# A preLN memory-attention and MLP kernel: how block 0's last-row values are laid out, pieces of the output weights, when norms and additions may start, and the length of a block's instruction stream

## The chip, the cores and the metric

The kernel runs on one core of a Trainium2 chip. The core has a matrix engine (PE, with its weight loads shown as PEld), a vector engine (DVE), an activation engine (ACT), a general engine (POOL) and an engine that issues DMAs (SP). Each runs its own list of instructions in order; they wait for one another through semaphores. The metric is the device time of one execution in microseconds, from runs on the chip. One execution was taken with the profiler.

## The reference

One sequence of 2048 tokens with 512 channels goes through an attention layer whose memory is carried from segment to segment, and then through an MLP, each behind a layernorm and with a residual:

```python
for s in range(n_seg):                                   # 64 segments of 32 tokens
    h = jnp.concatenate([mem, xs], axis=1)               # 8 memory rows + 32 tokens
    q, k, v = h @ Wq, h @ Wk, h @ Wv                     # 32 heads of 128
    p = softmax(where(mask, q k^T * scale, -1e9))
    o = einsum('bhte,hed->btd', p v, Wo)
    mem = o[:, :M, :]                                    # memory of the next segment
    outs.append(o[:, M:, :])
h  = x + A(layernorm(x))
h2 = h + (gelu(layernorm(h) @ w1 + b1) @ w2 + b2)        # 512 -> 1792 -> 512
```

The memory makes the segments a recurrence: segment s + 1 can't project its 8 memory rows before the output projection of segment s is done.

## The kernel before

**A planner.** The program is first recorded as a list of operations (`Sched.op`, L87), each with engine, duration, keys that it reads and writes, and, for PE, a place in a PE order that is written out by hand (`START` L50 for segment 0, `ORDER` L45 for the others). `schedule` (L166) lays the operations of the other engines out by a list scheduler: priority is the longest way to the end plus a bonus by the kind of result (`BONUS`, L31), and a copy that ACT or DVE could do (`either`) goes where it ends first. DMAs on SP are laid out with durations of 0.07 + KB/390 us (L142). `finalize` (L257) works out the semaphore waits: an operation waits for the last needed operation of each engine, unless its engine knows already that it is past. Waits beyond the first of a PE operation are moved up to an earlier operation without one, or become instructions of their own. `align` (L329) can put extra weight loads (pads) into the projection passes, so that the instruction count reaches a wanted phase modulo 256; before, `PHASE` is empty and only `LEAD` = 60 pads stand at the program's start.

**Segments and blocks.** Four segments make a block of 128 tokens (`bk`, `sg`). Each segment's pack A holds 24 rows of tokens and the 8 memory rows; the last 8 tokens of the four segments of a block are packed together as pack B and projected once a block. For segment s, PE runs (L45): passes of Q, K and V for both halves of the heads (`passes` L680, 4 matmuls of 512 columns for each of 4 channel chunks), scores SC (L826), the products PV for the memory and last rows (`pv_c` L863), PVA, the products of the 24 token rows of the segment before (`pv_a` L924), F, the projections of the next block's pack B, in segment 3 of a block instead the output projection of the last rows of the block before (`wo_B` L982), the output projection WO in two halves (`wo_units` L949), and the scores SA of the token rows (L892). WO's result is transposed into TT (L971), and two additions (L965) make the next segment's memory rows hT from it.

**Last-row values.** V of pack B comes as VSB, one row per token of the block. The products need it laid out in another way, VBD. `v_B_spread` (L783) writes VSB to a DRAM tensor v_last in four DMAs and reads it back in four others. For block 0 these eight DMAs are put by hand into SP's chain of weight loads (L1286): writes behind the fourth WK load, reads two WQ loads later.

**Weights.** WV, WK, WQ and WO come in four DMAs of 1 MB each (L606, L621). WO's unit q waits for two of the four pieces (L962). In START the WO of segment 0 is taken in two halves, with pack B's second Q projection and `warm`, 12 matmuls that compute nothing, between them.

**From attention to MLP.** `nat` (L998) puts a finished block together: a DMA transpose and four small DMAs into oN, on DVE the addition to x (L1006) and the statistics, on POOL rs2 (L1012, L1013), and a DMA to h_mid. While segments 54 to 60 run, `EARLY` (L43) starts the MLP of the first four blocks: `hx_early` (L1096) loads a row of h_mid into xT and normalizes it on DVE (L1098), `hn_early` (L1101) transposes the result by DMA; both wait for a named place in PE's order. Behind the last segment come w1 (L1109, L1317) and w2 (L1324) in four superblocks of 512 tokens. `p2_res` (L1063) adds b2 to the residual on POOL (L1066); it waits for all uses of WV and for rs2 of the last block. DVE adds this to PE's sum (L1387), and only then may PE use that bank for the next superblock.

Of the kernel before, what the change touches and what calls it, by code (L numbers as in the profile page):

```python
# [30 lines left out]
BONUS = {"": 5.14, "EC0": -5.14, "EC1": -4.67, "KA0": 6.35, "KA1": 9.81, "KB0": -1.33, "KB1": 2.96, "OTB": -1.22, "OTm0": 40, "OTm1": -40,  # L31
# [11 lines left out]
EARLY = {54: (("hx", 0, 0.1), ("hx", 1, 0.6)), 55: (("hn", 0, 0.1), ("hn", 1, 0.4), ("hx", 2, 0.8)), 56: (("hx", 3, 0.3), ("hn", 2, 0.7)),  # L43
         57: (("hn", 3, 0.1), ("w1", 0, 0.6)), 58: (("w1", 6, 0.2),), 59: (("w1", 1, 0.1), ("w1", 2, 0.8)), 60: (("w1", 3, 0.2), ("w1", 4, 0.5), ("w1", 5, 0.8))}
# [10 lines left out]
class Op:  # L55
# [3 lines left out]
    def __init__(self, eng, fn, reads, writes, name, dur, mode):  # L59
# [15 lines left out]
class Sched:  # L75
# [181 lines left out]
    def finalize(self):  # L257
# [64 lines left out]
        for e in engs:  # L322
            c = 0
# [1122 lines left out]
```

## Time and profile before

| what | value |
|---|---|
| median of 3 runs | 868.45 us (867.11 to 869.06) |
| profiled execution, its own time | 870.69 us |
| its span, first to last instruction | 869.0 us |
| mean granted PE clock | 0.984 |
| idle time of DVE, ACT | 32%, 38% of the span |
| bytes read from and written to HBM | 31.34 and 8.39 MB |
| first TT transpose, last one of 66 | at 53.8 us, at 771.8 us |

The profile's page gives busy time by engine, the DMA rate in slices and the costliest groups. The table of waits tells for each engine which line waited and what ended the wait; "issue" stands where no semaphore that the profile shows ended it. The chain of waits follows the work that ended last back through what released it. A timeline lists instructions in order of time, with the idle time before them and its releaser in brackets.

### The profile page before, as it was taken

How to read it: one execution, taken by the hardware profiler on the slowest of the kernel's cores; microseconds unless marked ns; L12 is line 12 of the kernel's file. 1: busy time of each engine (PE TensorE's matmuls, PEld its weight loads, DVE VectorE, ACT ScalarE, POOL GpSimd, SP SyncE). 2: the span in 40 equal slices, each digit the busy share in tenths (PEclk: the TensorE clock that was granted, in tenths of full speed). 3: DMA queues.
4: the chain of work that ended last, by engine and by line, in shares of the span. 5: the costliest groups of instructions: out<-in, count | busy, mean ns of one | idle time of the engine just before them, and what ended most of it. 6: DMA issues, size and time to landing. Idle time of an engine off the chain costs nothing.

```text
span 869.0 us, 46364 instructions
## 1 busy us (share of the span) xinstructions
PE 810.0 (93%) x21588; PEld 408.0 (47%) x20389; DVE 587.9 (68%) x1852; ACT 542.8 (62%) x1570; POOL 87.0 (10%) x206
## 2 busy tenths in 40 slices
PE   4688999999999999999999999999998999987998
PEld 1244454445455555454555545544553544442443
DVE  3277778788787878787878787777776878634111
ACT  2346676767676767676767776767775776632332
POOL 3021000101000000000000101000000000006200
PEclk9799999999999999999999999999999999998999
DMA  9961010201010111111110111010112130363200
GB/s 351 356 180 21 4 34 17 41 17 40 18 31 26 29 29 28 30 24 33 21 38 19 40 19 33 13 32 11 35 41 47 34 96 16 77 184 91 61 25 25
DMA packets 68033, 49.27 MB, mean 57 GB/s; under 512 B 29044, under 2 KB 64252, under 8 KB 67836
## 3 DMA queue, kind: packets, MB, share of 16 engines
q1 hardware_dynamic: 67504, 46.03, 18.9%
q8 instruction: 165, 2.70, 1.3%
q10 hardware_dynamic: 332, 0.27, 0.1%
q14 instruction: 32, 0.26, 0.1%
HBM read 31.34 MB, written 8.39 MB: 46 GB/s over the span
## 4 chain that ended last, share of the span: by engine, by line
PE 82%; DMA 6%; DVE 5%; ACT 3%; issue 2%; SPq 1%; POOL 1%; ACTq 0%; DVEq 0%
PE ps L695 37%; PE ps L959 14%; PE ps L447 7%; PE quad L1324 4%; PE ps L1317 4%; PE ps L988 3%; PE quad L871 3%; PE quad L840 2%; PE ps L902 2%; DMA WK<-in_B_w_dram 2%; PE quad L931 2%; PE ps L840 1%; ACT kq L713 1%; DMA WQ<-in_A_Wq_dram 1%; POOL WV L1066 1%
## 5 line engine op out<-in xcount | busy, mean ns | idle before, releaser
L959 PE MATMUL ps<-WO,OT 128*32 128x256 bf16 x4224 | 142.7, 275 | 6.8 <-issue 4.2
L713 ACT CAST OT<-quad 128x128 bf16<-128x128 f32 x191 | 84.0, 440 | 96.5 <-PE quad L875 96.0
L959 PEld LDWEIGHTS ps<-WO,OT 128*32 128x32 bf16 x4224 | 104.3, 97 | 55.6 <-DVE rsc L856 25.1
L695 PE MATMUL ps<-WQ,hT 128*32 128x512 bf16 x1796 | 123.4, 385 | 5.0 <-DVE hT L965 4.6
L695 PE MATMUL ps<-WK,hT 128*32 128x512 bf16 x1544 | 121.3, 385 | 0.0
L695 PE MATMUL ps<-WV,hT 128*32 128x512 bf16 x1528 | 118.5, 380 | 0.0
L713 ACT CAST kq<-ps 128x512 bf16<-128x512 f32 x158 | 92.4, 585 | 40.2 <-PE ps L695 39.5
L714 ACT ACTIVATE kq<-ps 128x512 bf16<-128x512 f32 x160 | 94.4, 590 | 24.5 <-PE ps L695 24.3
L736 DVE STREAM_TRANSPOSE KALL<-kq 128x256 f32<-128x256 f32 x160 | 69.0, 438 | 23.6 <-ACT kq L713 22.8
L971 DVE STREAM_TRANSPOSE TT<-ps 128x256 f32<-128x256 f32 x66 | 29.7, 450 | 79.7 <-PE ps L959 79.5
L757 POOL COPY ZC<-QTB 128x256 bf16<-128x256 bf16 x64 | 26.4, 414 | 509.9 <-PE ps L840 319.1
L695 PEld LDWEIGHTS ps<-WQ,hT 128*32 128x32 bf16 x1796 | 45.4, 97 | 54.4 <-issue 22.3
L1320 ACT ACTIVATE WQ<-ps,b1t 128x512 bf16<-128x512 f32 x42 | 28.9, 687 | 62.8 <-PE ps L1317 62.8
L736 DVE STREAM_TRANSPOSE QT<-kq 128x256 f32<-128x256 f32 x128 | 57.0, 445 | 15.5 <-ACT kq L714 10.9
L695 PEld LDWEIGHTS ps<-WK,hT 128*32 128x32 bf16 x1544 | 40.6, 98 | 55.8 <-issue 40.2
L695 PEld LDWEIGHTS ps<-WV,hT 128*32 128x32 bf16 x1528 | 40.3, 97 | 52.0 <-issue 29.5
L447 PE MATMUL ps<-WV,hT 128*32 128x512 bf16 x520 | 53.4, 382 | 0.0
L1387 DVE TENSOR_TENSOR WV<-quad,WV 128x512 bf16<-128x512 f32 x16 | 11.1, 692 | 62.5 <-PE quad L1324 54.9
L447 PE MATMUL ps<-WK,hT 128*32 128x512 bf16 x504 | 51.1, 381 | 0.0
L853 ACT ACTIVATE EC<-ps,nmc 128x64 f32<-128x64 f32 x130 | 39.5, 309 | 18.5 <-DVE nmc L849 18.4
L1324 PE MATMUL quad<-WK,WQ 128*128 128x512 bf16 x164 | 42.5, 388 | 5.5 <-DVE WV L1387 5.3
L713 DVE CAST VS<-ps 128x512 bf16<-128x512 f32 x64 | 42.8, 669 | 5.5 <-PE ps L447 5.5
(154 smaller groups left out, 1398.0 us busy)
## 6 DMA issues: line engine op xcount, KB each, us to landing
WV<-in_A_Wv_dram SPq DMA_DIRECT2D x4, 1024.0 KB, 12.7
WK<-in_A_Wk_dram SPq DMA_DIRECT2D x4, 1024.0 KB, 18.2
v_last<-VSB SPq DMA_DIRECT2D x64, 64.0 KB, 2.1
WQ<-in_A_Wq_dram SPq DMA_DIRECT2D x4, 1024.0 KB, 7.9
VBD<-v_last SPq DMA_DIRECT2D x64, 64.0 KB, 2.0
WO<-in_A_Wo_dram SPq DMA_DIRECT2D x4, 1024.0 KB, 15.2
h_mid<-xr SPq DMA_DIRECT2D x16, 128.0 KB, 1.8
WQ<-h_mid SPq DMA_DIRECT2D x4, 512.0 KB, 4.2
```

The costliest lines, as they stand in the source:

```text
L447: return e.add_instruction(mybir.InstMatmult(name="I-%d" % (4000000 + _kept[0]), engine=mybir.EngineType.PE, start_tensor_calc=start, stop ...
L695: ins = e.matmul(o, l, m, start=(k == 0), stop=(k == DC - 1), tile_position=(0, 32 * j), skip_group_check=True)
L713: return {"act": (lambda e: e.copy(out, src), t_act(n, ps_)), "dve": (lambda e: e.tensor_copy(out, src), 0.16 + 1.042e-3 * n * fast)}
L714: return {"act": (lambda e: e.mul(out, src, scale_), t_act(n, ps_)), "dve": (lambda e: e.tensor_scalar(out, src, scale_, None, ALU.mult), ...
L736: S.op("dve", lambda e: e.transpose(out, src), reads=[("kq", i)], writes=[key], dur=t_dve(256) + 0.02)
L757: S.op("pool", lambda e: e.tensor_copy(dst, src), reads=[("QTB", bk % 2, q) for q in range(2)], writes=[("ZCb", par)], dur=0.45)
L853: ins = e.activation(EC[:, r, sl, :], o[:, 64 * sl:64 * sl + 64], ACTF.Exp, bias=nmc[:, r, sl:sl + 1], accum_out=smc[:, r, sl:sl + 1])
L959: ins = e.matmul(ps[bank][32 * j:32 * j + 32, 0:256], lhs(slot(h)), wo_cols(h, b), start=(k == 0), stop=(k == 15), tile_position=(0, 32 * ...
L971: S.op("dve", lambda e: e.transpose(tt.rearrange("p c q t -> p (c q t)"), ps[bank][:, 0:256]), reads=[("ps", bank)], writes=[("TT", par)], ...
L1317: ins = e.matmul(ps[bank][:, 0:SBT], W1[:, cc, fc * P:(fc + 1) * P], hnT_of(k)[:, cc, :], start=(cc == 0), stop=(cc == DC - 1))
L1320: S.op("act", lambda e: e.activation(gT[:, fc, :], ps[bank][:, 0:SBT], ACTF.Gelu_apprx_tanh, bias=b1t[:, fc:fc + 1], scale=1.0), reads=[(" ...
L1324: S.op("pe", lambda e: e.matmul(quad[:, t, :], gT_of(k, fc)[:, t * P:(t + 1) * P], W2[:, fc, :], start=(fc == 0), stop=(fc == FC - 1)), re ...
```

## The change

Last-row values of block 0 are now laid out by PE. POOL builds masks of ones (`turn`, in the unused half of OTB), and 16 matmuls with them move VSB's rows to their places; two copies bring the result to VBD. The eight DMAs of block 0 are gone from SP's chain; the other blocks keep theirs. WO comes in eight pieces of 512 KB, and each WO unit waits for the two pieces that it reads; START takes segment 0's WO in four parts, with 8 + 8 warm matmuls. `pv_a` becomes two operations, each waiting for its own half of V. The early norm moves from `hx_early` to `hn_early`, with a PE place of its own, and the loads start at segment 51. The b2 additions of superblock 0 no longer wait for rs2. The planner gets SP durations for each kind of DMA (`occ`), drops waits that another wait of the same operation implies, and has new bonuses for nearly every kind; `align` pads the PE stream at the first segment of each block from block 1 on to the phase 92, so that a block is a multiple of 256 instructions, and `LEAD` is 0. `JOIN` and `RECORD` are empty: what they would switch stays off.

```diff
+TURN = 1.27
-PHASE = ()
+LOCK = 92
+JOIN = 0
+RECORD = ()
-LATE, RAW, LEAD = 0, 10, 60
+LATE, RAW, LEAD = 0, 10, 0
-BONUS = {"": 5.14, "EC0": -5.14, "EC1": -4.67, "KA0": 6.35, "KA1": 9.81, "KB0": -1.33, "KB1": 2.96, "OTB": -1.22, "OTm0": 40, "OTm1": -40,
+BONUS = {"": 40, "EC0": -0.86, "EC1": 0.35, "KA0": -40, "KA1": 2.87, "KB0": -40, "OTB": -0.07, "OTm0": 0.99, "OTm1": -3.04, "OTx": -40, "PA": -19.24,
...
-EARLY = {54: (("hx", 0, 0.1), ("hx", 1, 0.6)), 55: (("hn", 0, 0.1), ("hn", 1, 0.4), ("hx", 2, 0.8)), 56: (("hx", 3, 0.3), ("hn", 2, 0.7)),
-         57: (("hn", 3, 0.1), ("w1", 0, 0.6)), 58: (("w1", 6, 0.2),), 59: (("w1", 1, 0.1), ("w1", 2, 0.8)), 60: (("w1", 3, 0.2), ("w1", 4, 0.5), ("w1", 5, 0.8))}
+EARLY = {51: (("hx", 0, 0.2),), 52: (("hn", 0, 0.2), ("hx", 1, 0.6)), 53: (("hn", 1, 0.2), ("hx", 2, 0.6)), 54: (("hn", 2, 0.2), ("hx", 3, 0.6)),
+         55: (("hn", 3, 0.2),), 57: (("w1", 0, 0.6),), 58: (("w1", 6, 0.2),), 59: (("w1", 1, 0.1), ("w1", 2, 0.8)), 60: (("w1", 3, 0.2), ("w1", 4, 0.5), ("w1", 5, 0.8))}
-START = (("B", "V", 0, (0, 6), (1, 7)), "V", "X", ("B", "V", 1, (0, 6), (1, 7)), ("B", "K", 0, (0, 4), (1, 6)), "K0", "K1", ("B", "K", 1, (0, 4), (1, 6)),
-         ("B", "Q", 0, (0, 5)), "Q0", ("B", "Q", 0, (1, 4)), "Q1", "Z", "SC0", "SC1", ("B", "Q", 1, (0, 5)), "PV0", "PV1", "SA", "WO", ("T", "WO", 0, 4),
-         ("B", "Q", 1, (1, 6)), ("W", 7, 12), ("T", "WO", 4, 8))
+START = (("B", "V", 0, (0, 6), (1, 7)), "V", "Y", "X", ("B", "V", 1, (0, 6), (1, 7)), ("B", "K", 0, (0, 4), (1, 6)), "K0", "K1", ("B", "K", 1, (0, 4), (1, 6)),
+         ("B", "Q", 0, (0, 5)), "Q0", ("B", "Q", 0, (1, 4)), "Q1", "Z", "SC0", "SC1", ("B", "Q", 1, (0, 5)), "PV0", "PV1", "SA", "WO", ("T", "WO", 0, 2),
+         ("B", "Q", 1, (1, 6)), ("T", "WO", 2, 4), ("W", 7, 8), ("T", "WO", 4, 6), ("W", 7, 8), ("T", "WO", 6, 8))
...
-        o = self.op(eng, fn, reads, writes, {"sp": 0.07 + kb / 390.0, "act": 0.1}.get(eng, 1.0), 0, name, list(after) + [old])
+        o = self.op(eng, fn, reads, writes, {"sp": max(occ, 0.07 + kb / 390.0), "act": 0.1}.get(eng, 1.0), 0, name, list(after) + [old])
...
+            waits = [p for p in waits if not any(q is not p and snap[q][p.eng] >= p.idx for q in waits)]
...
-            if PHASE and o.tag is not None and o.tag[0] != seg:
+            if LOCK is not None and o.tag is not None and o.tag[0] != seg:
                 seg = o.tag[0]
-                owed = (PHASE[seg % 4] - at) % FETCH_N
-                if owed > FETCH_N - SLIP:
-                    owed = 0
+                if seg % 4 == 0:
+                    owed = (LOCK - at) % FETCH_N
+                    if owed > FETCH_N - SLIP:
+                        owed = 0
...
         for g in range(4):
-            load(lambda e, g=g: e.dma_start(WO[:, g * 8:(g + 1) * 8, :], wo_d[:, g * 8:(g + 1) * 8, :]), 1180, [("WO", g)])
+            for a in range(2):
+                h0 = 16 * (g // 2) + 8 * a + 4 * (g % 2)
+                load(lambda e, h0=h0: e.dma_start(WO[:, h0:h0 + 4, :], wo_d[:, h0:h0 + 4, :]), 590, [("WO", g, a)])
...
-            if r == 1:
+            if r == 1 and bk > 0:
                 v_B_spread(bk)
...
+        def turn_masks():
+            S.op("pool", lambda e: e.memset(turn[:], 0.0), writes=TURN_KEYS, dur=0.6)
+            for sg in range(4):
+                v = turn[:, sg, 24:152].rearrange("p (j c) -> p j c", j=4)[:, :, 0:8]
+                S.op("pool", lambda e, v=v, sg=sg: e.affine_select(v, v, pattern=[[-32, 4], [-1, 8]], compare_op=ALU.not_equal, fill=1.0,
+                                                                   base=-8 * sg, channel_multiplier=1), reads=TURN_KEYS, writes=TURN_KEYS, dur=0.2)
+
+        def v_turn():
+            for half in range(2):
+                for sg in (2 * half, 2 * half + 1):
+                    def f(e, sg=sg, half=half):
+                        for i in range(4):
+                            ins = e.matmul(quad[:, half, 256 * (sg % 2):256 * (sg % 2) + 256], turn[:, sg, 24 - 8 * i:152 - 8 * i], VSB[:, i].rearrange("p r e -> p (r e)"),
+                                           start=(i == 0), stop=(i == 3), skip_group_check=True)
+                        return ins
+                    S.op("pe", f, reads=TURN_KEYS + [("VSB", r) for r in range(2)], writes=[("ps", half)], dur=0.43, mode=MF, ni=8)
+                S.either(copy2(VBD[:, 0, 2 * half:2 * half + 2].rearrange("p s r e -> p (s r e)"), quad[:, half, :], 512), reads=[("ps", half)],
+                         writes=[("VBD", 0, j) for j in range(4)])
...
-            S.op("pe", f, reads=[("VS", par, 0), ("VS", par, 1), ("PTA", s % 2)], writes=QK, dur=0.26, mode=MR, ni=64)
+                S.op("pe", f, reads=[("VS", par, half), ("PTA", s % 2)], writes=QK, dur=0.13, mode=MR, ni=32)
...
-                S.op("pe", f, reads=[("WO", 2 * (q // 4) + g) for g in range(2)] + reads(q // 4), writes=[("ps", bank)], dur=0.22, mode=MC, ni=16)
+                S.op("pe", f, reads=[("WO", q // 2, a) for a in range(2)] + reads(q // 4), writes=[("ps", bank)], dur=0.22, mode=MC, ni=16)
...
-                     writes=[("hb", k % 2, t)], after=used["WV"] + S.users([("rs2", NTB - 1)]), dur=1.1)
+                     writes=[("hb", k % 2, t)], after=used["WV"] + (S.users([("rs2", NTB - 1)]) if k else []), dur=1.1)
...
             S.dma(lambda e: e.dma_start(xT_row, hd[:, t, :]), 128, reads=[("hd", t)], writes=["xT"], after=after)
+
+        def hn_early(t, after):
             S.op("dve", lambda e: e.tensor_scalar(xn[:, t % 2, :], xT_row, agg2[:, t, 0:1], rst2[:, t:t + 1], ALU.subtract, ALU.mult),
-                 reads=["xT", ("ag2", t), ("rs2", t)], writes=[("hn0", t), ("xn", t % 2)], dur=0.4)
-
-        def hn_early(t, after):
-            S.dma(lambda e: e.dma_start_transpose(hnT0[:, :, t * P:(t + 1) * P], xn[:, t % 2, :]), 256, reads=[("xn", t % 2)], writes=[("hnT", "first", t)], after=after)
+                 reads=["xT", ("ag2", t), ("rs2", t)], writes=[("hn0", t), ("xn", t % 2)], dur=0.4, after=after)
+            S.dma(lambda e: e.dma_start_transpose(hnT0[:, :, t * P:(t + 1) * P], xn[:, t % 2, :]), 256, reads=[("xn", t % 2)], writes=[("hnT", "first", t)], after=after, occ=TURN)
...
-                chain[10:10] = spread["in", 0]
-                chain[8:8] = spread["out", 0]
                 chain += spread["out", 1] + spread["in", 1]
...
```

More of the change, by code (lines that the diff above doesn't have):

```diff
@@ L66, in __init__ @@
         self.dma_sem = None
+        self.occ = self.kb = 0.0
         self.rank = self.start = 0.0
@@ L730, in build_kernel, with kq_T @@
         WKQ = ((WK, "WK"), (WQ, "WQ"))
[L732 removed]
+        zc, ve = [None, None], [None, None]
+        def kq_T(i, bank, out, key, scale_=None, after=()):
             S.either(copy2(kq[:, i], ps[bank][:, :].rearrange("p (a b e) -> p a e b", a=8, b=2), 512, True, scale_), reads=[("ps", bank)], writes=[("kq", i)])
             src = kq[:, i].rearrange("p a e b -> p a (e b)").bitcast(F32)
[L736 removed]
+            S.op("dve", lambda e: e.transpose(out, src), reads=[("kq", i)], writes=[key], dur=t_dve(256) + 0.02, after=after)
         def words(v):
@@ L749, in q_seg @@
             src = QT[:, 8 * r:8 * r + 8, NA:SEG, :].rearrange("p a t b -> p a b t")
-            S.either({"act": (lambda e: e.copy(dst, src), 0.31), "dve": (lambda e: e.tensor_copy(dst, src), 0.25)}, reads=[("QT", r)], writes=[("ZCm", s % 2, r)])
+            zc[r] = S.either({"act": (lambda e: e.copy(dst, src), 0.31), "dve": (lambda e: e.tensor_copy(dst, src), 0.25)}, reads=[("QT", r)],
+                             writes=[("ZCm", s % 2, r)])
         def qb_fill(s):
@@ L860, in sc_softmax @@
             S.op("dve", lambda e: e.transpose(PTC[:, r].rearrange("p t a -> p (t a)").bitcast(F32), PC[:, r].rearrange("p t a -> p (t a)").bitcast(F32)),
-                 reads=[("PC", r)], writes=[("PTC", r)], dur=0.24)
+                 reads=[("PC", r)], writes=[("PTC", r)], dur=0.24, after=[ve[0]] if JOIN & 2 and s > 0 and r == 0 else ())
         def pv_c(s, r):
@@ L880, in pv_c @@
             ot = OT[:, par, :, NA:SEG].rearrange("p (j r i) q -> p r j i q", r=2, i=4)[:, r]
-            S.either(copy2(ot, src[:, :, :, 0:MEM], 128), reads=QK, writes=[("OTm", par, r)])
+            S.either(copy2(ot, src[:, :, :, 0:MEM], 128), reads=QK, writes=[("OTm", par, r)], after=[ve[1]] if JOIN & 4 and s > 0 and r == 0 else ())
         def pv_c_b(s):
@@ L990, in f @@
                     return ins
-                S.op("pe", f, reads=[("WO", g) for g in range(4)] + [("OTB", bk % 2, sg) for sg in range(4)], writes=[("ps", bank)], dur=0.216, mode=MC, ni=8)
+                S.op("pe", f, reads=[("WO", g, a) for g in range(4) for a in range(2)] + [("OTB", bk % 2, sg) for sg in range(4)], writes=[("ps", bank)], dur=0.216, mode=MC, ni=8)
             okeys = [("OTB", bk % 2, sg) for sg in range(4)]
@@ L1000, in nat @@
             S.dma(lambda e: e.dma_start_transpose(oN[:], opT[:, bk % 2].rearrange("p c t -> p (c t)")), 256,
-                  reads=[("opA", bk % 2, k) for k in range(4)] + ["opT0"], writes=["oN"])
+                  reads=[("opA", bk % 2, k) for k in range(4)] + ["opT0"], writes=["oN"], occ=TURN)
             rows = oN[:].rearrange("p c t -> p (c t)")
             for sg in range(4):
-                S.dma(lambda e, sg=sg: e.dma_start(rows[32 * sg + NA:32 * sg + SEG, :], oBn[8 * sg:8 * sg + 8, :]), 8, reads=["oBn", "oN"], writes=[("oNr", sg)])
+                S.dma(lambda e, sg=sg: e.dma_start(rows[32 * sg + NA:32 * sg + SEG, :], oBn[8 * sg:8 * sg + 8, :]), 8, reads=["oBn", "oN"], writes=[("oNr", sg)], occ=0.62)
             xs = xr[:, bk % XR, :]
@@ L1071, in p2_T @@
                 S.dma(lambda e, t=t: e.dma_start_transpose(hnT_of(k)[:, :, t * P:(t + 1) * P], xn2[:, k % 2, t, :]), 256, reads=[("xn4", bf_of(k), t)],
-                      writes=[("hnT", bf_of(k), t)], after=used["WQ"])
+                      writes=[("hnT", bf_of(k), t)], after=used["WQ"], occ=TURN)
         NP = FC // 2
@@ L1130, in gT_keys @@
             return gT0_home[fc // 2][1] if k == 0 else [("gT", fc)]
+        turn = view(OTB, H * 32, [P, 4, 152])
+        TURN_KEYS = [("OTB", 1, sg) for sg in range(4)]
+        turn_masks()
         build_masks(4, 5)
@@ L1292, in build_kernel @@
             last = {n: i for i, (n, _, _) in enumerate(ORDER)}
-            for i, (n, _, _) in enumerate(ORDER):
-                if last[n] == i:
-                    S.tag = (s, n)
-                    part(n)
+            for n in RECORD or [n for i, (n, _, _) in enumerate(ORDER) if last[n] == i]:
+                S.tag = (s, n)
+                part(n)
             for n, lo, hi in ORDER:
```

45 lines of the change are left out of this document (23 added, 22 removed), and 10 rows, old and new, of the table BONUS.

## The prediction

> **What bounds the kernel now.** I read the page first, then the table of waits on PE, then the chain of waits and the timelines of the places that this table names.
>
> ```profile
> span 869.0 us, 46364 instructions
> ...
> PE 810.0 (93%) x21588; PEld 408.0 (47%) x20389; DVE 587.9 (68%) x1852; ACT 542.8 (62%) x1570; POOL 87.0 (10%) x206
> ...
> q8 instruction: 165, 2.70, 1.3%
> ```
>
> PE is the bound: no other engine is busy for more than 68% of the span. What can be won without taking work from PE is PE's idle time, and the speed that it loses after long idle times. The row of queue q8 is PE's program: 2.70 MB in 165 packets, 16 KB or 256 instructions of 64 bytes each. Now the waits of PE (engine line, waited for: total us, times, longest):
>
> ```profile
> PE quad L871 <- DVE PTC L860: 6.2, 15, 0.4
> PE quad L1324 <- DVE WV L1387: 5.3, 4, 3.4
> PE ps L695 <- DVE hT L965: 4.6, 4, 2.1
> ...
> PE ps L959 <- issue: 4.2, 6, 1.1
> ...
> PE ps L695 <- issue: 1.6, 3, 0.7
> ```
>
> Each is one mechanism. The 15 waits for PTC are one per block of four segments. The four for L1387 stand at the end of the recurrence. The longest for hT is at segment 55. "issue" means that no semaphore held PE: its instructions had not come. The change has a part for nearly every row. I go by place.
>
> **The start.** The chain of waits in the first 75 us, the DMA rate of the same 75 us in 40 slices of 1.875 us, and two rows of SP's timeline:
>
> ```profile
> 20.10 6.97 DMA v_last<-VSB
> ...
> 29.43 10.18 DMA WQ<-in_A_Wq_dram
> ...
> 50.24 2.54 PE ps L664 x11
> 52.78 1.02 PE ps L959 x32
> 53.82 0.45 DVE TT L971
> ```
> ```profile
> GB/s 2 229 324 397 419 411 409 409 400 411 419 402 386 395 410 408 199 269 367 401 369 348 349 347 348 351 353 290 154 42 134 46 6 73 40 30 70 9 0 9
> ```
> ```profile
> 27.15 1.77 SPq L793 DMA_DIRECT2D VBD<-v_last  x4
> 28.96 0.95 SPq L609 DMA_DIRECT2D WQ<-in_A_Wq_dram  x2
> ```
>
> SP issues in order. The four reads of v_last wait for its writes, which land at 20.10 + 6.97 = 27.07, and the last two WQ loads stand behind these reads until 28.96. So the rate falls to 199 and 269 GB/s in two slices. Without the detour there is no such hole: (410-199) + (410-269) = 352 GB/s over 1.875 us is 0.66 MB, or 1.6 us at 410 GB/s. The eight 64 KB transfers, 0.52 MB, are also gone: 1.3 us. WQ, now complete at 29.43 + 10.18 = 39.61, should be complete some 2.9 us earlier, and segment 0's chain with it. In its place PE gets 16 matmuls of 256 columns. At half of the 231 ns of a 512-column one (2.54 us / 11) they take 1.8 us, before the WQ data can be there, so I cost them, their two copies and POOL's five mask instructions at nothing; if that cover were gone, they would cost about 3 us. They add a wait on PE, for the copies of VSB; behind it stand tile 1's transposes and the K projections, and segment 0's V projection runs between copies and wait. But START now spends 16 warm matmuls instead of 12 inside WO: 4 x 231 ns = 0.9 us more on PE. WO in eight pieces doesn't bind: 4.19 MB at the 349 GB/s that the row shows for WO take 12.0 us from 36.7, to 48.7, and the last WO units would run at about 52.8 - 2.0. **Term: 2.9 - 0.9 = 2.0 us gained** (bounds 0 and 2.9).
>
> [...]
>
> **The stalls called issue.** They sum to 4.2 + 1.6 = 5.8 us. Two of them, from the timeline:
>
> ```profile
> 584.31 1.04 PE L695 MATMUL ps<-WK,hB 128*32 128x512 bf16 x13 [0.61 <-issue]
> ```
> ```profile
> 606.65 0.83 PE L695 MATMUL ps<-WV,hB 128*32 128x512 bf16 x12 [0.66 <-issue]
> ```
>
> A segment of the code before is 639 PE instructions: 636 by its loops with the weight loads that are skipped, and 3 separate waits. A block is 2556, so its place against the 256-instruction packets moves by 4 from block to block. The stalls come where a packet's end falls just behind the short instructions from PVA to F1: PVA, PV, WO, F and SA are 400 of the 639 instructions and take less than half of the segment. The lock pads a block to 2560, so that one phase holds for all. By before's count of 639 the four segments of a block would begin at 92, 219, 90 and 217. Counting on through the program, the odd segments of before passed the phases 80 to 134 without an issue stall of 0.3 us. 217 and 219 are just those of segments 50 and 48, at whose ends the two rows above stand; 213 and 221 to 229 were passed without one. The new code's count isn't known to me: it drops waits that others imply, and splits PVA's. One or two waits fewer move these phases and the places of the WO waits off the bad pair. **Term: 5.8 us gained** (bounds: 5.8 gained, and the rivals below). The pads themselves, 4 weight loads in a block, lie under 512-column matmuls: nothing, and at most 15 x 0.1 us uncovered. Splitting PVA moves no work: its first half may run before the second V copy, and PE shows no idle time before PVA now.
>
> [...]
>
> **The order on DVE.** Segment 16, the first of its block:
>
> ```profile
> 221.59 0.68 DVE L996 TENSOR_TENSOR oBn<-OTB 32x512 bf16<-32x512 f32 x1
> ```
> ```profile
> 226.74 0.27 PE L871 MATMUL quad<-PTC,VS 32*128 32x16 bf16 x16 [0.44 <-DVE PTC L860]
> ```
>
> DVE does the block's slow addition L996 at the segment's beginning, and the softmax behind it comes 0.44 us late. The priorities are new throughout; that of oBn falls from -0.37 to -40, which lets the list scheduler put L996 behind the softmax. I can't see the order that results. If it does, 15 x 0.4 = 6.2 us go; if other orders get worse by as much, 6.2 are lost. I take half: **3.1 gained**.
>
> **The early norms.** Segments 54 and 55:
>
> ```profile
> 651.06 1.06 PE L695 MATMUL ps<-WQ,hT 128*32 128x512 bf16 x16
> ...
> 662.21 0.41 DVE L1098 TENSOR_SCALAR xn<-xT,agg,rst 128x512 bf16<-128x512 bf16 x1 [3.60 <-DMA xT<-h_mid]
> ...
> 664.11 1.90 PE L695 MATMUL ps<-WQ,hT 128*32 128x512 bf16 x16 [2.14 <-DVE hT L965]
> ```
>
> DVE stands 3.60 us on a norm whose row comes late, because SP was itself waiting on v_last; TT and hT queue behind it, PE stops for 2.14, and its next 16 matmuls take 1.90 instead of 1.06. The change puts the norm with the transpose, 0.6 of a segment (6 us) behind the load, three segments earlier. Such a load lands in about 2 us:
>
> ```profile
> xT<-h_mid SPq DMA_DIRECT2D x4, 128.0 KB, 2.1
> ```
>
> So DVE no longer waits; next is PE itself. **Term: 2.1 + 0.8 = 2.9 gained** (bounds 0 and 2.9). The moved DMAs are the same eight; all but the last transpose now pass SP ahead of the v_last copies of segment 54, on which it waited.
>
> **The end.** First DVE and PE behind the last segment, then the chain:
>
> ```profile
> 761.16 0.43 DVE L1006 TENSOR_TENSOR xr<-xr,oN 128x512 bf16<-128x512 bf16 x1 [3.14 <-DMA oN<-oBn]
> ...
> 762.25 1.18 PE L1109 MATMUL ps<-hnT,hT 128*128 128x512 bf16 x4 [3.13 <-DVE QTB L713]
> ```
> ```profile
> 785.34 7.82 POOL WV L1066 x7
> 795.72 1.71 PE ps L1317 x4
> 797.43 1.71 PE quad L1324 x4
> 799.13 1.63 PE ps L1317 x4
> ```
>
> At 762 DVE again stands on a DMA, with PE's evacuation behind it. The new SP costs (1.27 for a transpose, 0.62 for a small copy) tell the scheduler that this DMA is late, so it should put ready work first. Then ACT, full of gelus, is next late. Between 0 and 3.1 I take **1.5 gained**. At 785 POOL starts the b2 additions, all of them held until the last block's norm (rs2), and PE waits 5.3 us in all for the output additions behind them. Then PE is slow: 12 matmuls take 1.71 + 1.71 + 1.63 = 5.05 us, against 12 x 0.231 = 2.8. For the first four tiles the change drops this hold; their rows are loaded long before and POOL is idle, so 4 x 1.1 us are done before 762. DVE then adds when PE's sums are done. The other four tiles may start at 785 as before and are needed a superblock later. **Term: 5.3 + 2.3 = 7.6 gained** (bounds 5.3 and 7.6).
>
> **Sum.** 2.0 + 5.8 + 3.1 + 2.9 + 1.5 + 7.6 = 22.9 us. The profiled execution took 870.69 us (span 869.0), so 847.8 by its own time. It is 2.2 above the median of the runs, 868.45; against the median the sum gives **845.5 us**.
>
> **Rivals.**
> - *The lock doesn't hold* (the count misses instructions, and the phase drifts on): the term 5.8 is gone, 851.3. For it: the count is the program's own estimate. Against: 165 packets are just its length.
> - *The additions stay late*, behind another instruction on POOL: 845.5 + 7.6 = 853.1. Against: POOL is 10% busy.
> - *The lock pins the stall* in two segments of four, at 217 and 219: 30 x 0.63 = 18.9 us, 864.4. For it: the two rows at these phases. Against: each needs the packet's end within 2 or 3 instructions.
> - *PTC late everywhere*: the new order brings the 0.44 us to all 63 segments, 27.7 us in place of 3.1: 870.1, no change. Against: three of four segments have none.
> - *The lock pins it in all four segments*, the one that ends slower: 60 x 0.63 = 37.8, 883.3. It decides from 22.9 / 60 = 0.38 us a segment. Against: two of the four phases were passed clean.
>
> **How the numbers follow.** Chances: forecast 0.63, no lock 0.10, late additions 0.08, pinned in two 0.11, PTC everywhere 0.04, pinned in four 0.04. The forecast's bounds: all terms at their best are 2.9 + 5.8 + 6.2 + 2.9 + 3.1 + 7.6 = 28.5, 840; the priorities are new everywhere, so 837 at the low end. At the high end the start, the order and the 762 wait at nothing, with the lock or the additions failing, are 6.6 and 5.8 to 7.6 above the forecast: 859. The range 837 to 859 holds the first three cases, 0.81. A measurement tells 0.2% (1.7 us) from no change. Faster: 0.63 + 0.10 + 0.08 + 0.11 = 0.92; within 0.2%: 0.04; slower: 0.04.
>
> **What would show it.** WQ landed by 37 and TT of segment 0 near 52 instead of 53.8. No issue rows of 0.3 us and more in the waits; q8 packets at the same places of each block. No wait of L871 for PTC. Segment 55 as long as 54. L1066 near 750, no wait of L1324 for L1387. I am wrong if issue rows come once or twice in each block, if DVE's new order makes PE wait in every segment, or if the start's gain is eaten by warm matmuls.

## The result and the profile after

The changed kernel takes 842.22 us in the median of 4 runs (840.98 to 842.46), the kernel before 868.75 us in the runs beside them (867.11 to 873.33): a ratio of 0.968, 95% interval [0.965, 0.972]. The forecast was 845.5 us, range 837 to 859. The profiled execution has a span of 840.7 us, 28.3 less than before, where the prediction's sum was 22.9.

From the page after, span and engines:

```profile
span 840.7 us, 46469 instructions
...
PE 800.1 (95%) x21625; PEld 396.3 (47%) x20613; DVE 577.3 (69%) x1920; ACT 554.3 (66%) x1504; POOL 91.6 (11%) x211
...
q8 instruction: 165, 2.70, 1.4%
```

PE has 9.9 us less busy time, with 37 matmuls more (21625 against 21588). So part of the gain is not idle time that vanished but matmuls that ran faster. The granted clock of PE stood at 0.50 in six stretches before, 27.3 us in all; after, it does so in two, 6.8 us in all. The waits of PE after (total us, times, longest):

```profile
PE ps L831 <- POOL maskL L572: 11.3, 1, 11.3
PE quad L901 <- DVE PTC L890: 7.6, 31, 1.4
...
PE ps L703 <- DVE hT L996: 3.2, 4, 1.0
...
PE ps L1140 <- ACT VSB L721: 1.1, 1, 1.1
...
PE ps L990 <- issue: 0.2, 1, 0.2
```

Line numbers have moved: L871 is now L901, L860 L890, L695 L703, L959 L990, L971 L1002, L965 L996, L996 L1027, L1109 L1140, L1317 L1350, L1324 L1357, L1387 L1420. Three entries of before are gone: the issue waits of the prediction (5.8 us, now 0.2), the output additions (5.3), and the 2.1 us wait for hT. One has not gone: PTC, 6.2 us in 15 places, is 7.6 in 31. The longest wait of all, for maskL, is new in its size and costs nothing: it lies at the very start, where WQ's arrival decides (PE waits 1.98 us for it at 37.06). Before's list has one more issue row in the attention part, which the prediction left out (its 0.7 us are in segment 4, the rest in segment 64):

```profile
PE ps L902 <- issue: 1.0, 2, 0.7
```

To see where the 28.3 us lie I cut both spans at the transposition TT that ends each segment (L971 before, L1002 after):

| stretch | before | after | gained | forecast |
|---|---|---|---|---|
| start to TT of segment 0 | 54.27 | 52.70 | 1.6 | 2.0 |
| to TT of segment 59 | 654.46 | 638.25 | 16.2 | 11.8 |
| segments 60 to 63 | 43.92 | 46.12 | -2.2 | |
| segments 64 and 65 | 19.66 | 15.76 | 3.9 | 1.5 |
| to the end | 96.7 | 87.9 | 8.8 | 7.6 |

A second cut turned out to be the most telling. Segments 8 to 59 are 13 blocks of four. I take the shortest of each of the four places in a block as what the plan can do, and count as **excess** what all others take above it:

| kernel | shortest four, sum | excess, 13 blocks |
|---|---|---|
| before | 11.10 + 10.66 + 10.66 + 10.67 = 43.09 | 17.8 |
| after | 11.07 + 10.84 + 10.67 + 10.67 = 43.25 | 1.4 |

The best block has become 0.16 us longer. All that these segments gained is regularity: after, the 13 blocks take 43.26 to 43.47 us each, before they took 43.16 to 45.87.

The start, from PE's timeline after (start, duration, line, idle time before and its cause):

```profile
37.06 1.05 PE L703 MATMUL ps<-WQ,hB 128*32 128x512 bf16 x8 [1.98 <-DMA WQ<-in_A_Wq_dram]
...
41.32 0.30 PE L870 MATMUL ps<-KALL,ZC 128*32 128x64 bf16 x16 [1.17 <-ACT ZC L760]
...
43.67 0.28 PE L901 MATMUL quad<-PTC,VS 32*128 32x16 bf16 x16 [0.62 <-ACT ps L845]
...
44.19 1.06 PE L990 MATMUL ps<-WO,OT 128*32 128x256 bf16 x16
...
47.37 1.90 PE L672 MATMUL ps<-WV,ident 128*128 128x512 bf16 x8
49.20 0.62 PE L990 MATMUL ps<-WO,OT 128*32 128x256 bf16 x16
49.75 1.90 PE L672 MATMUL ps<-WV,ident 128*128 128x512 bf16 x8
51.58 0.62 PE L990 MATMUL ps<-WO,OT 128*32 128x256 bf16 x16
```

WQ is complete at 37.06 instead of the 39.61 worked out for before, and WO's first group starts at 44.19. The two groups of eight warm matmuls stand between the last WO groups. The waits at 41.32 and 43.67 come just ahead of the second of these windows, which give the clock (length, busy time and count by engine, granted clock, DMA share, GB/s):

```profile
36.68:40.09 3.41, 3.03 (x40) 1.04 (x40) 0.45 (x1) 0.82 (x2) 0.74 (x2) 0.50 1.10 349
43.51:46.92 3.41, 3.25 (x89) 2.22 (x93) 2.22 (x7) 1.21 (x4) 0.00 (x0) 0.50 1.12 351
```

These are the two stretches at a granted clock of 0.50 that remain; behind them it stays at 1.00. Before had three stretches of this kind in the start (25.73 to 32.56, 39.38 to 42.80 and 46.21 to 49.62), one at segment 56 (from 664.02), one from 763.01 to 766.42, and one near the end:

```profile
793.73:800.56 6.83, 6.06 (x14) 2.05 (x15) 3.25 (x8) 0.69 (x1) 1.35 (x2) 0.50 0.44 135
```

This slow stretch is the second part of what the late b2 additions cost. POOL and PE after:

```profile
733.18 4.55 POOL L1097 TENSOR_TENSOR WV<-WQ,b2bc 128x512 f32<-128x512 bf16 x4 [20.33 <-DMA WQ<-h_mid]
...
774.80 8.92 POOL L1097 TENSOR_TENSOR WV<-WQ,b2bc 128x512 f32<-128x512 bf16 x8
```
```profile
764.36 4.66 PE L1350 MATMUL ps<-WQ,WK 128*128 128x512 bf16 x20
768.86 1.03 PE L1357 MATMUL quad<-WK,WQ 128*128 128x512 bf16 x4
769.72 1.03 PE L1350 MATMUL ps<-WQ,WK 128*128 128x512 bf16 x4
```

The first four b2 additions are over before 738, and PE's groups of four matmuls follow each other every 0.86 us where the chain of before had 1.7.

### The profile page after: what moved, and what is told of

Read it like the earlier page. It is cut to its first block, busy times and chain, and to the rows that moved or that the text cites. A ratio compares the mean times of both kernels' runs of the same rounds, so it can differ in the third digit from the quotient of the medians.

```text
span 840.7 us, 46469 instructions
## 1 busy us (share of the span) xinstructions
PE 800.1 (95%) x21625; PEld 396.3 (47%) x20613; DVE 577.3 (69%) x1920; ACT 554.3 (66%) x1504; POOL 91.6 (11%) x211
## 4 chain that ended last, share of the span: by engine, by line
PE 79%; DVE 11%; ACT 4%; DMA 3%; SPq 2%; issue 1%; DVEq 0%
PE ps L703 35%; PE ps L990 11%; PE ps L453 7%; PE quad L1357 6%; PE ps L1350 4%; PE quad L901 3%; PE ps L1019 3%; DMA WQ<-in_A_Wq_dram 2%; SPq L615 2%; PE quad L962 2%; PE quad L870 2%; PE ps L932 2%; DVE opT L996 2%; DVE PC L889 1%; PE ps L870 1%
## 5 line engine op out<-in xcount | busy, mean ns | idle before, releaser
L990 PE MATMUL ps<-WO,OT 128*32 128x256 bf16 x4224 | 140.3, 274 | 3.2 <-ACT OT L721 1.5
L990 PEld LDWEIGHTS ps<-WO,OT 128*32 128x32 bf16 x4224 | 103.8, 96 | 52.3 <-ACT VS L721 26.6
L721 ACT CAST OT<-quad 128x128 bf16<-128x128 f32 (+1 forms) x130 | 68.3, 526 | 87.5 <-PE quad L905 86.9
L703 PE MATMUL ps<-WQ,hT 128*32 128x512 bf16 x1796 | 121.3, 383 | 3.4 <-DVE hT L996 3.2
L721 ACT CAST kq<-ps 128x512 bf16<-128x512 f32 x162 | 94.7, 585 | 42.1 <-PE ps L703 41.4
L703 PE MATMUL ps<-WK,hT 128*32 128x512 bf16 x1544 | 117.0, 379 | 0.0
L703 PE MATMUL ps<-WV,hT 128*32 128x512 bf16 x1528 | 116.8, 380 | 0.0
L721 ACT CAST VS<-ps 128x512 bf16<-128x512 f32 x127 | 74.8, 589 | 12.9 <-PE ps L703 11.0
L768 POOL COPY ZC<-QTB 128x256 bf16<-128x256 bf16 x64 | 28.3, 442 | 498.3 <-PE ps L870 360.1
L1002 DVE STREAM_TRANSPOSE TT<-ps 128x256 f32<-128x256 f32 x66 | 29.7, 450 | 67.8 <-PE ps L990 66.4
L703 PEld LDWEIGHTS ps<-WQ,hT 128*32 128x32 bf16 x1796 | 44.7, 97 | 50.4 <-issue 20.9
L703 PEld LDWEIGHTS ps<-WV,hT 128*32 128x32 bf16 x1528 | 36.8, 97 | 56.1 <-issue 42.7
L703 PEld LDWEIGHTS ps<-WK,hT 128*32 128x32 bf16 x1544 | 38.0, 97 | 53.2 <-issue 39.5
L453 PE MATMUL ps<-WV,hT 128*32 128x512 bf16 x520 | 51.3, 382 | 0.0
L944 ACT ACTIVATE SA<-SA 128x256 f32<-128x256 f32 x64 | 26.7, 417 | 35.9 <-DVE SA L943 35.9
L453 PE MATMUL ps<-WK,hT 128*32 128x512 bf16 x504 | 49.8, 379 | 0.0
L1420 DVE TENSOR_TENSOR WV<-quad,WV 128x512 bf16<-128x512 f32 x16 | 11.1, 691 | 54.4 <-PE quad L1357 54.4
L889 DVE TENSOR_TENSOR PC<-EC,rsc 128x128 bf16<-128x128 f32 x128 | 40.1, 313 | 4.3
## 6 DMA issues: line engine op xcount, KB each, us to landing
WK<-in_A_Wk_dram SPq DMA_DIRECT2D x4, 1024.0 KB, 15.8
```

The costliest lines, as they stand in the source:

```text
L453: return e.add_instruction(mybir.InstMatmult(name="I-%d" % (4000000 + _kept[0]), engine=mybir.EngineType.PE, start_tensor_calc=start, stop ...
L703: ins = e.matmul(o, l, m, start=(k == 0), stop=(k == DC - 1), tile_position=(0, 32 * j), skip_group_check=True)
L721: return {"act": (lambda e: e.copy(out, src), t_act(n, ps_)), "dve": (lambda e: e.tensor_copy(out, src), 0.16 + 1.042e-3 * n * fast)}
L768: S.op("pool", lambda e: e.tensor_copy(dst, src), reads=[("QTB", bk % 2, q) for q in range(2)], writes=[("ZCb", par)], dur=0.45)
L889: S.op("dve", lambda e: e.tensor_tensor(PC[:, r].rearrange("p t a -> p a t"), EC[:, r], bc, ALU.mult), reads=[("EC", r), ("rsc", r)], writ ...
L990: ins = e.matmul(ps[bank][32 * j:32 * j + 32, 0:256], lhs(slot(h)), wo_cols(h, b), start=(k == 0), stop=(k == 15), tile_position=(0, 32 * ...
```

## Experiments

Each kernel below is the changed kernel with the edit shown. Medians are of 4 to 6 runs. Kernels that share a series share its runs of before (medians 866.98 to 867.48 us).

**The b2 hold back (x_gate).**

```diff
-  after=used["WV"] + (S.users([("rs2", NTB - 1)]) if k else [])
+  after=used["WV"] + S.users([("rs2", NTB - 1)])
```

> The changed kernel, with the b2 additions of superblock 0 held again until rs2 of the last block. Theory (the hold is what costs, by PE's idle time behind it and by the slow clock that follows): L1066 starts some 1 us after rs2 again, PE waits about 5.3 us at L1357 for L1420, matmuls behind it run at half speed for 2 to 3 us, and the time is 842.2 + 7.6 to 8.8, so 850 to 851. Rival (the order of the new plan has made room, so that the hold no longer decides): 842 to 844, no wait of L1357 over 1 us.

849.51 us (847.20 to 852.32), ratio 0.980 [0.976, 0.984]. From its waits and from POOL's timeline:

```profile
PE quad L1357 <- DVE WV L1420: 5.4, 4, 3.6
```
```profile
771.37 8.91 POOL L1097 TENSOR_TENSOR WV<-WQ,b2bc 128x512 f32<-128x512 bf16 x8
```

Wait and half clock (6.83 us from 774.57) are both back; the end takes 97.0 us, as before. The median is 7.3 us above the changed kernel's first series and 6.1 above its second; between the two traces the end differs by 9.1. The mechanism is shown. Its size by the medians, 6 to 7 us, is somewhat below the 7.6 to 8.8 that was expected.

**The changed kernel again (x_again)**, as a yardstick for the runs beside it.

> The changed kernel once more, unedited, as the yardstick of the runs beside it. Expected: 842 us, within 2 us, and a span near 841 with segment 0's TT at 52.7, segments of 11.07, 10.85, 10.68 and 10.68 us in each block, and waits for PTC of some 7.6 us in 31 places. If the places of the PTC waits or the lengths of the segments were another draw, they would not be an effect of the order.

843.44 us (842.96 to 844.95), ratio 0.974 [0.970, 0.979], span 841.4, excess 0.9. The two series of the same kernel lie 1.2 us apart.

**Start: the detour back (x_dram)** (V values of block 0 through DRAM, no turn matmuls or masks).

```diff
-  if r == 1 and bk > 0:
+  if r == 1:
       v_B_spread(bk)
...
+  chain[10:10] = spread["in", 0]
+  chain[8:8] = spread["out", 0]
```

> The changed kernel with block 0's V values sent through DRAM again, as before: eight transfers in SP's queue, no turn matmuls and no turn masks on POOL. Theory: these reads hold back the last WQ loads, which come some 2.6 us later, and segment 0's TT with them, to about 55.3 instead of 52.7; the whole takes 2 to 3 us longer. Rival: the WQ loads don't set the end of segment 0 in the changed kernel, because maskL, which the 11.3 us wait names, comes earlier without the turn masks and PE works ahead: within 0.5 us of the changed kernel.

845.87 us (844.75 to 846.85), ratio 0.976 [0.972, 0.980]: 2.4 us more than the changed kernel beside it. SP's and PE's timelines:

```profile
27.86 1.76 SPq L823 DMA_DIRECT2D VBD<-v_last  x4
29.67 0.95 SPq L615 DMA_DIRECT2D WQ<-in_A_Wq_dram  x2
```
```profile
40.94 0.62 PE L703 MATMUL ps<-WQ,hB 128*32 128x512 bf16 x8 [1.99 <-DMA WQ<-in_A_Wq_dram]
```

The last WQ loads again stand behind the reads, and the last pass starts 3.9 us later. In this trace TT of segment 0 even ends at 57.05, because the half clock also holds for 10.24 us from 41.98. The rival (WQ not the bound) falls.

**Start: fewer warm matmuls (x_warm4b).**

```diff
-  ("T", "WO", 2, 4), ("W", 7, 8), ("T", "WO", 4, 6), ("W", 7, 8), ("T", "WO", 6, 8)
+  ("T", "WO", 2, 4), ("W", 7, 4), ("T", "WO", 4, 6), ("W", 7, 4), ("T", "WO", 6, 8)
...
-  "SC0", "SC1"
+  "SC0", ("W", 4, 5), "SC1"
```

> The changed kernel with 8 of the 16 warm matmuls inside WO of segment 0 taken out (4 after each of the two places instead of 8) and 5 put into the wait ahead of the second score group, where PE stands idle before the half clock at 43.5 us. What is left out computes nothing. Theory: the 8 stand on the path and take 8 x 0.24 = 1.9 us; the 5 lie in PE's idle time and keep its clock up through 43.5, worth up to 1.7 us more: 1.9 to 3.5 us faster than the changed kernel, TT of segment 0 at 49.2 to 50.8. Rival: the warm matmuls fill a wait for the last pieces of WO, or keep the clock from falling to half for 3.4 us, and without them the time goes to that wait or clock: no gain.

841.43 us (840.46 to 842.32), ratio 0.971 [0.967, 0.975]: 2.0 us less than the changed kernel beside it, and the two ranges of times don't touch (against its first series it is 0.8 us less). This is the fastest version. Its window and its last wait in the start:

```profile
43.50:46.90 3.40, 2.25 (x100) 1.73 (x100) 2.10 (x8) 2.35 (x8) 0.00 (x0) 1.00 1.10 350
```
```profile
49.81 0.62 PE L990 MATMUL ps<-WO,OT 128*32 128x256 bf16 x16 [0.20 <-DMA WO<-in_A_Wo_dram]
```

The clock no longer falls at 43.5, and TT of segment 0 ends at 50.92. In ten of the eleven other traces with the START of the changed kernel a stretch at 0.50 begins between 41.87 and 44.12, and in the eleventh (x_plan) one lasts from 37.37 to 47.61; so its absence here is hardly chance. But both edits were made at once: eight matmuls fewer on the path are 8 x 0.24 = 1.9 us by themselves, and what the clock adds was not separated. Against the three of those traces that have, like this one, a single stretch at half clock in this part (x_nolock, x_lock219 and x_order87, TT at 51.4 to 51.6), TT is only 0.5 to 0.7 us earlier. Taking out still more would not help, for the last WO group now waits 0.20 us for its data. That wait also tells when WO is complete, about 49.8, so that the eight pieces didn't bind in the changed kernel, where this group starts at 51.58. WO in four pieces was not tried.

The stretches at 0.50 for which this document gives the length or both ends lasted 3.41, 6.83 or 10.24 us.

**The lock taken out (x_nolock).**

```diff
-LOCK = 92
+LOCK = None
```

> The changed kernel without the lock: no pads, so a block is 4 x 637 = 2548 instructions and its phase moves by 8 from block to block. Theory (PE stalls at a packet's end at some phases only): issue waits of 0.3 to 1.1 us come back at some of the segments, 2 to 6 us in all, 844 to 848. Rival (a packet's end is hidden, and it was the new order that took the issue waits away): 842.2 within 1 us and no issue wait over 0.25 us.

844.82 us (843.89 to 846.03), ratio 0.975 [0.972, 0.978]: 1.4 to 2.6 us above the two medians of the changed kernel. Excess 3.7 us instead of 1.4 or 0.9, nearly all in odd segments (17, 27, 29, 31 and 35 by 0.5 to 0.8 each). So with the new order the drift costs 2.3 to 2.8 us by the traces, not 5.8; the ratios alone (0.975 against 0.968 and 0.974) would not show it. The trace counts 2549 PE instructions in a block, so the phase moves by 11 from block to block, not by 8.

**The lock at the pair that I had suspected (x_lock219).** `LOCK = 219`.

> The changed kernel with the phase 219 in place of 92, which puts the first WO instruction of each block's first segment 3 instructions behind a packet's end, counted as in the kernel before, where the first WO instructions 2 and 4 behind it went with the stalls of 0.61 and 0.66 us. Theory (it is this place that stalls): about one issue wait of 0.6 us in each of 15 blocks, 9 us, 851; at least 845. Rival (those two stalls had other causes, and a fixed phase of any size is as good): 842 to 843.

847.31 us (846.76 to 848.97), ratio 0.978 [0.975, 0.981].

```profile
PE ps L703 <- issue: 2.5, 3, 1.5
```

The place matters: excess 5.0. But with the same place in every block, only segments 29, 37, 49 and 57 among the second of their blocks are long (by 0.5 to 1.9), the others not at all. The theory that one place of the packet's end costs 0.6 us in each block falls. The changed kernel itself comes within an instruction of the place: its first segments have 649 PE instructions by the trace and the others 637, so if the first begins at 81 (see x_lock97 below), the second begins at 218. A stall at the end of the second would lengthen the third, and the 13 third segments have 0.2 us of excess in all. Not all of this run's loss lies at that place: segment 63, where the clock is at 0.50 from 738.19 to 741.61, is 1.0 us longer than in the changed kernel.

**The old priorities (x_order)**, all else as changed: the table BONUS of before.

> The changed kernel with the priorities (the table BONUS) of the kernel before, all other parts kept. Theory: of the 15.3 us that segments 3 to 59 gained, the lock has about 3 and the end of the stall at segment 55 about 4; the rest, some 5 to 8 us, is the new order of the small operations, not the waits for PTC. Then this kernel takes 5 to 8 us more than the changed one, spread over the ordinary segments, which are longer by 0.1 us each in the mean. Rival 1: the order is worth nothing, because the old priorities do as well under the new costs and the new split of PVA: within 2 us. Rival 2: the priorities were worked out for just this kernel, and the old ones are far off: 10 us and more lost, with waits in every segment.

848.59 us (846.46 to 851.56), ratio 0.980 [0.975, 0.984]: 5.2 us more than the changed kernel beside it. Its best block is shorter, 11.14 + 10.63 + 10.63 + 10.66 = 43.06, but its excess is 7.5, most of it in the first segments of the blocks. Its waits, and PE at the beginning of segment 44:

```profile
PE quad L901 <- DVE PTC L890: 5.5, 15, 0.4
...
PE ps L1019 <- issue: 2.8, 4, 1.2
PE quad L901 <- issue: 1.7, 1, 1.7
```
```profile
520.64 1.55 PE L1019 MATMUL ps<-WO,OTB 128*32 128x512 bf16 x16
521.82 0.61 PE L932 MATMUL ps<-KALL,QT 128*32 128x32 bf16 x32
```

and at the same place of the changed kernel:

```profile
516.81 1.04 PE L1019 MATMUL ps<-WO,OTB 128*32 128x512 bf16 x16
517.67 0.42 PE L932 MATMUL ps<-KALL,QT 128*32 128x32 bf16 x32
```

No wait is named in segment 44, and yet the 16 matmuls take 0.51 us more and the 32 short ones 0.19. The records of the single matmuls show a stop inside the group: one of the 16 starts 0.51 us behind the one before it, the others 0.21. Such a stop lengthens the group and isn't in the list of waits. It ended 1.3 us after a packet of q8 had landed. The listed stops behave alike: before's ten issue waits over 0.3 us in segments 4 to 51, and the seven over 0.3 us of this run, all ended 1.2 to 1.6 us after a packet of q8 had landed and 2.2 to 3.0 us after it had begun. So I read these stops as waits for instructions; that q8 brings PE's fits its 2.70 MB, which are 64 bytes for each of the 42173 instructions that before's trace has of PE, its weight loads and separate waits. In the records of q8 the packet fetched last ahead of these first segments began 2.2 to 2.5 us before the segment where it was long by 0.3 us or more (one at 2.9), and 2.7 to 3.5 us before it in the others; in the changed kernel 2.7 to 3.5 in all.

**Is that the place of the packet's end (x_lock97, x_order87)?** `LOCK = 97` moves the changed kernel's places by 5 instructions, to where the old priorities have theirs; `LOCK = 87` with the old priorities moves these back.

> The changed kernel with LOCK = 97 in place of 92: every place against the packets moves by 5 instructions, so that the first segment of a block begins at 86 instead of 81, as it does in the run with the old priorities; work and order stay as they are. Theory: the packet whose 256 instructions end just behind the segment's beginning is the tight one. In the changed kernel its fetch begins 2.7 to 3.4 us ahead of the segment and only the later ones cost 0.16 us; with the old priorities it began 2.2 to 3.0 us ahead, and PE went on 2.7 to 2.9 us behind the fetch's start. So 5 instructions more bring 0.3 to 0.8 us of stall at the beginning of about 9 of the 15 blocks, at L1019 and the score matmuls behind it: 4 to 6 us slower than the changed kernel, near 848, q8's packet at -2.2 to -2.9. Rival: the stalls of that run came with the old order itself (other instructions in the same places), and 5 instructions are nothing: within 1 us of the changed kernel.

> The kernel with the old priorities again, with LOCK = 87 in place of 92, so that the first segment of a block begins at 81, as in the changed kernel. Theory: its 5 us over the changed kernel are stalls of that one packet, not the order. Its blocks without a stall are 11.15 + 10.63 + 10.63 + 10.67 = 43.1 us, against 43.3 of the changed kernel (11.07 + 10.85 + 10.68 + 10.69). Then most blocks take 43.1 to 43.3 us, and the whole is 3 to 6 us faster than with LOCK = 92: 842 to 845.5, no slower than the changed kernel. That would mean that the new order as such won nothing. Rival: the new order is what wins: still 847 to 849, with long segments elsewhere.

`LOCK = 97`: 842.36 us (841.25 to 842.59), ratio 0.971 [0.969, 0.974], excess 1.0. Old priorities with `LOCK = 87`: 849.54 us (847.11 to 854.01), ratio 0.981 [0.978, 0.984], excess 6.7, the packet again at 2.2 to 2.6 us in most blocks. Both expectations failed. Both rivals held in the time; but the long segments of the second run are again the first of their blocks (5.7 of the 6.7 us), not elsewhere as its rival had it. Five instructions are nothing; the stall goes with the priorities. Why these delay a fetch by 1 us stays open. They change the order of the operations on the other engines, but also PE's own stream: with the old ones PE has 2 or 3 separate wait instructions in each segment (163 in all; before, 194), with the new ones 1 or 2 (83). Whether it is these that hold the fetch back was not tried. SP's transfers of V values through DRAM run just then in both kernels, but stalls and their ends didn't match block by block.

**What took the stall at segment 55 away?** Three parts of the plan could have. First the old places of the early rows and norms (x_early: the table EARLY, and the norm again with its row):

> The changed kernel with the old places of the early norms: loads at segments 54 to 56, the norm in the load's own step. Theory (DVE in order stands on a late load, TT and hT behind it): one wait of DVE of 2 us or more for xT, one wait of PE for hT of 1 to 2.5 us in segment 55 or 56, PE at half speed behind it, 842.2 + 2.9 to 4.1, so 845 to 846.5. Rival (the new SP durations in the plan alone put the norm late enough): 842 to 843, no such wait.

844.35 us (842.30 to 845.09), ratio 0.974 [0.970, 0.977]; segments 55 and 56 take 10.83 + 11.07 us. No stall: the theory falls. Then these old places together with the old costs of SP's transfers (x_occ):

```diff
-  {"sp": max(occ, 0.07 + kb / 390.0), "act": 0.1}
+  {"sp": 0.07 + kb / 390.0, "act": 0.1}
```

> The changed kernel with the early rows and norms in the old places (as in the run before that had them and showed no stall) and, beside that, the scheduler's old costs for SP's transfers (no 1.27, 0.62, 0.6 or 0.43 us; 0.07 us and 390 bytes per ns for each). Only the plan differs, no work. Theory: the new costs are what kept the early norm from holding DVE and PE at segment 55. Without them the norm stands again too early in DVE's order: DVE waits 2 us and more on its row, PE 1 to 2 us behind it, and segment 55 takes 12 to 13 us instead of 10.7; the wait on DVE near 751 of 2 to 3 us comes back too. 4 to 8 us slower than the changed kernel. Rival: what took the stall away is the absence of the v_last detour or the other priorities: segment 55 stays below 11.3 us and the whole within 2 us.

843.09 us (840.84 to 844.23), ratio 0.972 [0.969, 0.974]; 10.85 + 11.21 us. No stall, the second theory falls too. Only segments 64 and 65 are longer, 17.6 us instead of 15.8. Last, these two and the old priorities together (x_plan):

> The changed kernel with three parts of the plan undone at once: the old priorities, the old places of the early rows and norms, and the scheduler's old costs for SP's transfers. Each of them alone left segment 55 without the stall of before (10.67 to 10.85 us). The work, the lock, the turned V values, the pieces of WO and the dropped hold stay as changed. Theory: any one of the three is enough to keep the early norm out of the way; with none of them the stall comes back: DVE waits 2 us or more on a row of h_mid, PE 1 to 2 us on hT behind it, segments 55 and 56 take 24 us and more together instead of 21.9. The stalls at the beginning of the blocks, as with the old priorities, come too, and the whole takes 849 to 853 us. Rival: something else of the change took the stall away (a block 2 us shorter at that place, fewer waits, the split of PVA), and the plan has no part in it: segments 55 and 56 stay at 21.6 to 22.2 us together, the whole at 847 to 849.

849.96 us (845.20 to 851.54), ratio 0.979 [0.975, 0.982]. The stall is back, on DVE and then on PE:

```profile
653.12 0.41 DVE L1129 TENSOR_SCALAR xn<-xT,agg,rst 128x512 bf16<-128x512 bf16 x1 [3.45 <-DMA xT<-h_mid]
```
```profile
655.04 1.05 PE L703 MATMUL ps<-WQ,hT 128*32 128x512 bf16 x16 [0.90 <-DVE hT L996]
```

Segment 55 takes 12.90 us; with segment 56 (11.04) the two are 23.94, just short of what was expected. So the new priorities alone keep the stall away (x_occ), and so do the other two together (in x_order segments 55 and 56 took 10.67 + 11.14). It came back when all three were undone; other pairs were not tried.

## Why the prediction was right, and where it was not

**The start: right, 1.6 against 2.0.** Both ends are single traces, though: TT of segment 0 ends at 51.4 to 51.6 in three traces with the changed START, which have one stretch at half clock there, and at 52.5 to 53.1 in the eight with two or a longer one. So against before's one trace the gain is 1.2 to 2.8. WQ came 2.6 us earlier (2.9 forecast), and x_dram shows that the detour was its cause. From WO's first group to the end of TT it is 52.70 - 44.19 = 8.5 us, 1.0 more than before: the warm matmuls (0.9 forecast). WO's pieces came at the row's rate, 349 and 351 GB/s in the two windows above, and WO was complete at about 49.8 (48.7 forecast).

**The issue stalls: gone, but the term was mis-sized and half of its cause was missed.** I took 5.8 us from the list of waits, without the row of L902, and gave them to the lock. The list is too short: a stall inside a group isn't in it. Of before's 17.8 us of excess, segments 55 and 56 have (13.31 - 10.67) + (12.70 - 11.10) = 4.2; the other 13.6 are more than twice the list, though how much of them is fetching wasn't separated. And the lock alone doesn't remove them: with the old priorities and the lock the excess is 7.5, with the new ones and no lock 3.7, with both 1.4. The two work together. The nearest to the lock without the new plan is x_plan: its excess is 11.0, or 8.8 without segments 55 and 56, where before has 13.6. So 4.8 us, not far from my term, went with what x_plan keeps of the change: the lock, the split of PVA and the dropped waits, of which the last two were undone in no run. That the pair 217 and 219 sets the stall was wrong as well: with 218 in the second segments of the changed kernel no stall follows, and 219 stalled 4 blocks of 13.

Little is left of these stalls in the changed kernel: over its 165 packets the list has 0.2 us of issue in the first trace and 1.5 in the second, and the excess in segments 8 to 59 is 1.4 and 0.9 us. With `LOCK = 219` a single issue wait took 1.5 us.

**The order on DVE: the step failed.** I expected the slow addition oBn behind the softmax and then no wait for PTC. The first came true, the second didn't. DVE and PE in the first segment of a block, after:

```profile
222.61 0.24 DVE L890 STREAM_TRANSPOSE PTC<-PC 128x64 f32<-128x64 f32 x1
222.88 0.68 DVE L1027 TENSOR_TENSOR oBn<-OTB 32x512 bf16<-32x512 f32 x1
```
```profile
222.91 0.26 PE L901 MATMUL quad<-PTC,VS 32*128 32x16 bf16 x16 [0.20 <-DVE PTC L890]
```

and in the second:

```profile
362.29 0.52 DVE L996 TENSOR_TENSOR opT<-TT 64x96 bf16<-64x96 f32 x2
362.82 0.17 DVE L886 RECIPROCAL rsc<-smc 128x2 f32<-128x2 f32 x1
363.02 0.30 DVE L889 TENSOR_TENSOR PC<-EC,rsc 128x128 bf16<-128x128 f32 x1
363.36 0.25 DVE L890 STREAM_TRANSPOSE PTC<-PC 128x64 f32<-128x64 f32 x1
```
```profile
363.67 0.26 PE L901 MATMUL quad<-PTC,VS 32*128 32x16 bf16 x16 [0.21 <-DVE PTC L890]
```

Another addition, opT, now stands right ahead of the softmax's second half, and PE waits 0.2 us for PTC twice in a block, in its first and second segment, where it waited 0.44 once. The wait moved from the first half of the softmax to the second. With the old priorities (x_order) it is back in one place a block, 0.4 us each. The term is not 3.1 but nothing; by the shortest blocks it is a loss of 0.16 us each. What the new order did bring (x_order: 5.2 us in the medians, 3.6 of them in segments 8 to 59) came with the stalls above, not with PTC.

**The early norms: right in what goes, wrong in why.** Segment 55 is 2.6 us shorter and 56 1.5, together 4.1 (forecast 2.9). I gave this to the norm's new place; undoing that place changed nothing, since the priorities alone are enough.

**The 762 wait and what is ahead of it: 3.9 - 2.2 = 1.7, forecast 1.5.** The sum is right by two errors. Segments 64 and 65 gained 3.9, more than my bound of 3.1: the wait itself fell from 3.1 to 1.1 us (the row of L1140 above), and the clock, at 0.50 behind it before, no longer falls there, which the term left out. Segments 60 to 63 lost 2.2, which no step foresaw; 1.4 of it is one wait in segment 63 that the list puts down to PTC. DVE does norms of the MLP there ahead of the softmax's second half, and its product PC takes 1.11 us beside POOL's first b2 additions, 0.30 where these come late (x_gate). But PTC is not the only cause: with the old priorities it is ready in time, and PE stops for 1.7 us at the same line, the second issue row of x_order, until 2.6 us after a packet of q8 began. The new costs of SP's transfers are worth some 1.9 of the 3.9 (x_occ against x_early, which has 15.8); the rest wasn't traced.

**The b2 additions: right.** 8.8 us in the profile, 6.1 to 7.3 in the medians, forecast 7.6 with bounds of 5.3 and 7.6. POOL ran them even earlier, at 733 instead of 750.

Of the rivals none came in full. The nearest was the lock that pins a stall: it took the old priorities or another number to show it. PTC late everywhere came in part, as 29 waits of 0.2 us in the segments behind the first, in place of 63 of 0.44.

## What to carry to other kernels

In a kernel of many equal stages, compare the stages with the shortest of their kind before reading the list of waits: 17.8 us of irregularity stood where the list named 5.8 for issue, and in segment 44 of x_order a stall inside a group of matmuls only made the group longer, by 0.51 us. The gate on a whole buffer's last norm cost twice here, by 5.3 us of waits and by the 6.83 us at a granted clock of 0.50 that began during them; drop such a gate for the part that doesn't need it. And undo parts of a plan one by one and together: here the priorities, and the other two parts together, each hid the same stall, so that undoing one part showed nothing.

## What was not expected of the hardware

With the packet's end at the same instruction in each block, the fetch began at times that differ by over 1 us from block to block (2.2 to 3.5 us ahead of the segment with the old priorities), and but for one stall of 0.3 us only the late ones, up to 2.5 us ahead, stalled PE by 0.3 us or more. And idle times as short as those at 41.32 and 43.67 (1.17 and 0.62 us) were followed by 3.41 us at a granted clock of 0.50: in the 3.42 us ahead of that stretch PE was busy for 1.54 us. With five matmuls of no use in the first of them (x_warm4b) PE was busy for 2.43 us of the same length, from 40.69, and the clock stayed at 1.00.
